# A Fourier layer with routed experts on one core: selection per batch, loads ahead of their use, folds two steps ahead, paired tiles

## The chip, the cores and the metric

The kernel runs on one core of a Trainium2 chip. The metric is the device time of one execution in microseconds (us); lower is better. Five engines work side by side, each in its own program order: TensorE (PE, with its weight loads shown as PEld), VectorE (DVE), ScalarE (ACT), GpSimd (POOL) and SyncE (SP), which here issues nearly all DMAs.

## The reference

There are 8 batches of 3136 rows of 256 numbers. Per batch:

```python
X = np.fft.rfft(x, axis=1)                 # along the 3136 rows
Yr = Xr @ w_r - Xi @ w_i + b_r
Yi = Xr @ w_i + Xi @ w_r + b_i
Y  = sign(Y) * max(abs(Y) - 0.01, 0)       # on Yr and Yi
y  = np.fft.irfft(Yr + 1j * Yi, n=3136, axis=1)
scores = y @ w_gate                        # one score a row
top = the 128 rows of the batch with the highest scores
y[top] += sigmoid(scores[top]) * (relu(y[top] @ w1) @ w2)   # w1 256x1024, w2 1024x256
```

## The kernel before

The transform of 3136 = 98 x 32 rows is done as two stages of matmuls with a pass through scratch memory between them, and so is the inverse. The units of work are these:

- `ld_x`, `fold`, `s1`: a batch comes in 8 groups. `ld_x` loads a group into one of four fixed tiles `xt` (batch 0 also uses the tiles `cv`), `fold` adds and subtracts its two halves into `sd` (POOL; every other group of batch 0 on DVE), `s1` runs the 98-point matmuls into the PSUM tile `s`, ACT copies that to `at`, and three DMAs store it to the scratch `As`.
- `ld_a`, `s2`: a batch has 13 frequency groups. `s2` runs the 32-point matmuls into `px`; ACT rounds the result to `Xh` (line 425) and DVE makes the rest `Xl` (line 426).
- `spectral`: the product of X and the weights in three real products of six matmuls each. The first, called k1, goes to one half of the PSUM tile `pc`; ACT copies it to `ks` (line 441), POOL adds the bias to give `kb` (line 443), and DVE adds `kb` to the other two products in `py` (line 446).
- `shrink` makes `Y` from `py` (ACT line 451, DVE line 453).
- `s2i`: the inverse 32-point matmuls, also into `pc` (line 470). ACT copies the result to `ct` (line 474), and two DVE operations reduce it against the gate (`junk`, line 477), which gives the part `Csc` of the scores. The result is stored to the scratch `Cs`.
- `ld_c`, `s1i`: 8 groups a batch, loaded from `Cs` into four tiles `cv`, matmuls into `s`, a copy to `ot` on ACT and three DMAs to the output.
- Routing: `score` makes a batch's scores, `select` finds the 128th highest by a search over the bits of the numbers, and `place` turns the threshold into 128 row numbers `idx`. One turn of the search compares all scores with several candidates (`c`, line 232), counts (`n`, line 237), sums over partitions by a matmul into the upper half of `pc` (`tot`, line 240), and updates the threshold by four small DVE operations (`ok`, `d`, `w`, `f`).
- Experts: `gather` fetches the 128 rows by an indirect DMA on POOL, `prepare`, `hidden` and `combine` run the two expert matmuls, and a second indirect DMA on POOL writes the rows back. This is called FFN below.

Every engine's order is written by hand. One loop runs over t, one spectral group a step; t = 0 to 103 are the 104 groups of the 8 batches. In step t the program emits, in this order: stores left from the step before; the loads; `s2` of group t+1; the first of the step's `s1`/`s1i` pairs (`s1` is 17 groups ahead, `LEAD`, and `s1i` 17 behind, `LAG`); one tick of the routing threads; `spectral` of t; the folds for the next step's `s1`; one tick of the FFN; `s2i` of t-1; `shrink` of t; a second pair if there is one; and a second tick of the routing threads. A tick runs each thread (a generator) to its next `yield`. After the last step the threads are ticked until they end.

Routing has four threads: batches 0 to 3 are selected together, then 4 and 5, then 6, then 7. A thread of several batches begins its search when the last of them has its scores. The search takes two bits a turn for several batches, with two ticks a turn, and three bits with one tick for a single one. The expert weights w2 come in 8 parts, one every second step from t = 22: a part is loaded and, in the same step, rounded by ACT (`w2h`, line 199) and split by POOL. Ahead of the loop stands a prelude: the loads of batch 0 and of the spectral weights, the splitting of those weights on DVE (`consts_a`), the 8 folds and `s1` of batch 0, and 50 matmuls that only keep TensorE busy (`warm`).

Of the kernel before, what the change touches and what calls it, by code (L numbers as in the profile page):

```python
# [23 lines left out]
NF = 64  # L24
# [76 lines left out]
def fourier_moe(ctx: ExitStack, tc: tile.TileContext, x, w_r, w_i, b_r, b_i, wg, w1, w2,  # L101
# [20 lines left out]
    xts, cvs = [[c_tile([128, 4, D], F32, n + str(k)) for k in range(4)] for n in ("xt", "cv")]  # L122
    for t in xts + cvs:
        nc.gpsimd.memset(t[32:64], 0.0)
    nc.scalar.dma_start(out=w, in_=t_w)
    g_sb = c_tile([128, NJ - 1, 3 * N2], F32, "g_sb")
    gt_sb = c_tile([NF, 3, NF], F32, "gt_sb")
    wts = [[c_tile([128, 2, D], F32R, n + c) for c in "hl"] for n in ("ws", "wd", "wn")]
    xth, xtl = [c_tile([128, 2, 3, 128], F32R, n) for n in ("xth", "xtl")]
# [15 lines left out]
    digits = c_tile([N1, 256], U32, "digits")  # L145
# [4 lines left out]
    route_ps = pc[:, 1, D:]  # L150

    def consts_a():
# [3 lines left out]
        ld(wi, w_i.rearrange("(h p) e -> p h e", p=128))  # L156

# [31 lines left out]
    def consts_b():  # L189
        ld(wq, t_wq)  # L190
        make_identity(nc, ident)

    def consts_moe(k):
        if k == 0:
            ld(w1s, w1.rearrange("(h p) f -> p h f", p=128))
        elif k <= FF // 128:
            t = pool.tile([128, D], F32, name="xe", bufs=3)
            ld(t, w2[128 * k - 128:128 * k])
            nc.scalar.copy(out=w2h[:, k - 1, :], in_=t)
            nc.gpsimd.tensor_tensor(out=w2l[:, k - 1, :], in0=t, in1=w2h[:, k - 1, :].bitcast(F32), op=ALU.subtract)  # L200
        else:
            ld(digits, t_dig)
            nc.gpsimd.dma_start(out=tm, in_=t_m)
            nc.gpsimd.iota(iota, [[1, 128 * NCHK]], base=0, channel_multiplier=0, allow_small_or_imprecise_dtypes=True)
            nc.gpsimd.iota(nrow, [[1, 1]], base=0, channel_multiplier=N2, allow_small_or_imprecise_dtypes=True)
            nc.gpsimd.iota(tcol, [[128, NCHK]], base=0, channel_multiplier=1, allow_small_or_imprecise_dtypes=True)
# [6 lines left out]
    def select(bs, bits, thrs):  # L213
        nb = bs.stop - bs.start
        tag = f"_{bs.start}"
        sv = scores[:, bs, :].rearrange("p b (o c) -> p b o c", o=1)
# [4 lines left out]
        for hi, i in zip([32] + cuts, cuts):  # L221
            m = 2 ** (hi - i) - 1
            f = pool.tile([N1, nb, m], U32, name="f" + tag, bufs=1)
            if w is None:
                nc.vector.memset(f, 0)
            else:
                nc.vector.tensor_tensor(out=f, in0=digits[:, 8 * i:8 * i + m].rearrange("p (o m) -> p o m", o=1).broadcast_to([N1, nb, m]),
                                        in1=w.broadcast_to([N1, nb, m]), op=ALU.bitwise_xor)
            if nb > 1:
                yield  # L230
            c = pool.tile([N1, nb, m, N2], BF16, name="c" + tag, bufs=1)
            nc.vector.tensor_tensor(out=c, in0=sv.broadcast_to([N1, nb, m, N2]),  # L232
                                    in1=f.bitcast(F32).rearrange("p b (m o) -> p b m o", o=1).broadcast_to([N1, nb, m, N2]),
                                    op=ALU.is_ge)
            n = pool.tile([N1, nb, m], BF16, name="n" + tag, bufs=1)
            with nc.allow_low_precision(reason="counts up to 28 are exact"):
# [4 lines left out]
            w2 = pool.tile([N1, nb, 1], U32, name="w" + tag)  # L241
            if w is None:
                nc.vector.tensor_scalar(out=w2.bitcast(I32), in0=tot, scalar1=cap - 0.5, scalar2=1.0, op0=ALU.is_ge, op1=ALU.subtract)
            else:
                d = pool.tile([N1, nb, 1], U32, name="d" + tag, bufs=1)
                if m == 1:
                    nc.vector.tensor_scalar(out=d, in0=tot, scalar1=cap - 0.5, scalar2=None, op0=ALU.is_ge)
                else:
                    ok = pool.tile([N1, nb, m], F32, name="ok" + tag, bufs=1)
# [5 lines left out]
        for b in range(bs.start, bs.stop):  # L255
            thrs[b] = w.bitcast(F32)[:, b - bs.start, :]

    def place(b, thr, slots):
# [4 lines left out]
        yield  # L263
        pt = route_ps[:2 * N2, :N1]
        nc.tensor.matmul(pt, mf, eye, start=True, stop=True)
        mt = pool.tile([2 * N2, N1], BF16, name="mt")
        nc.vector.tensor_copy(mt, pt)
        yield
# [6 lines left out]
        for a in range(2):  # L275
            nc.vector.tensor_copy(row[:, a, N2 + 1:], nrow)
        yield
# [6 lines left out]
        for k in range(NCHK):  # L284
# [7 lines left out]
            yield  # L292
# [11 lines left out]
            slots[b, k] = idx  # L304

# [54 lines left out]
    def ld_x(b, i):  # L360
        t = xt[b, i] = (cvs if b == 0 and i > 3 else xts)[i % 4].rearrange("p (h c) d -> p h c d", h=2)
        for r in range(2):
            ld(t[64 * r:64 * r + 48], xv[b, :48, :, 4 * i + 2 * r:4 * i + 2 * r + 2, :])
        ld(t[48:113:64], xv[b, 48, :, 4 * i:4 * i + 4, :].rearrange("h (r c) d -> r h c d", r=2))

    def fold(b, i):
        t = xt.pop((b, i)).rearrange("p h c d -> p h (c d)")
        f = sd[b, i] = pool.tile([128, 2, 2 * D], F32, name="sd", bufs=2)
        for k, op in enumerate((ALU.add, ALU.subtract)):
            (nc.vector if b == 0 and i % 2 else nc.gpsimd).tensor_tensor(out=f[:113, k], in0=t[:113, 0], in1=t[:113, 1], op=op)  # L370

    def s1(b, i):
        if i == 0:
            As[b] = dram.tile([2, NH, N2, D], F32, name="As")
        f = sd.pop((b, i))
        p = ps.tile([128, 2, 2 * D], F32, name="s", bufs=1)
        for r in range(2):
            for c in range(2):
                nc.tensor.matmul(p[64 * c:64 * c + 64, r, :], w[64 * r:64 * r + NH, c, :], f[64 * r:64 * r + NH, c, :], start=True, stop=True)  # L379
        t = pool.tile([128, 4, D], F32, name="at", bufs=3)  # L380
        nc.scalar.copy(out=t.rearrange("p (r c) d -> p r (c d)", r=2), in_=p)  # L381

        def store():
            for q in range(2):
                nc.sync.dma_start(out=As[b][q, :48, 4 * i:4 * i + 4, :], in_=t[64 * q:64 * q + 48])
            nc.sync.dma_start(out=As[b][:, 48, 4 * i:4 * i + 4, :], in_=t[48:113:64])
        stores.append(store)

    def ld_a(b, g):
        if g == G - 1:  # L390
            av[b, g] = pool.tile([64, 1, D], F32, name="av", bufs=3)
# [295 lines left out]
```

## Time and profile before

| | us |
|---|---|
| median of 3 runs | 1042.05 (1038.84 to 1045.21) |
| the profiled execution's own time | 1035.69 |
| its span | 1033.9 |

| engine | busy share of the span | instructions |
|---|---|---|
| PE | 76% | 7540 |
| PEld | 54% | 7540 |
| DVE | 43% | 1275 |
| ACT | 36% | 579 |
| POOL | 30% | 268 |

The busy shares are means over stretches with different limits, so they do not say what a change to one stretch is worth. The granted clock of TensorE over the execution was 0.892 of 2.4 GHz; at each moment it is either 1.2 or 2.4 GHz. `kb` (line 443) runs once in each of the 104 steps, so counting it counts steps.

### The profile page before, as it was taken

What the parts mean: (1) busy time and instruction counts of PE and PEld (TensorE: products, weight loads), DVE (VectorE), ACT (ScalarE), POOL (GpSimd) and SP (SyncE); (2) the same over time, 40 slices, a digit from 0 to 9 for tenths busy, and PEclk for the clock granted to TensorE, in tenths of its full rate; (3) what the DMA queues carried; (4) which work ended last, traced back from release to release, by engine and by line L of the source; (5) the groups of instructions that cost most, each with busy time, mean ns of one, the idle gap of its engine ahead of it and who ended that gap; (6) DMA issues with size and microseconds to landing.
All of it is one profiled execution on the core that took longest, in us unless ns stands there. A gap on an engine that the chain in (4) does not pass through costs nothing. (4 is left out here: it accounts for less than half of the span.)

```text
span 1033.9 us, 19572 instructions
## 1 busy us (share of the span) xinstructions
PE 782.4 (76%) x7540; PEld 557.1 (54%) x7540; DVE 447.1 (43%) x1275; ACT 369.7 (36%) x579; POOL 312.6 (30%) x268
## 2 busy tenths in 40 slices
PE   1589998965865789988777878678878766677675
PEld 0066666643643466666555655466556655564364
DVE  1214454522322344543555454544554466544521
ACT  0214453523433345553443343433443222223211
POOL 5125644423322353433333233331411110111011
PEclk9999999987888799998899798997998877888799
DMA  8378967875675687997685576864553334315520
GB/s 182 93 184 206 242 175 172 262 196 139 154 180 140 160 216 203 251 246 179 162 212 160 130 191 171 215 162 110 154 154 95 98 99 114 88 52 142 165 60 21
DMA packets 104762, 163.69 MB, mean 158 GB/s; under 512 B 12161, under 2 KB 65502, under 8 KB 104670
## 3 DMA queue, kind: packets, MB, share of 16 engines
q1 hardware_dynamic: 103630, 160.18, 59.7%
q0 software_dynamic: 896, 2.17, 0.7%
q8 instruction: 60, 0.98, 0.4%
q14 instruction: 32, 0.26, 0.1%
q10 hardware_dynamic: 144, 0.10, 0.0%
HBM read 84.35 MB, written 78.12 MB: 157 GB/s over the span
## 5 line engine op out<-in xcount | busy, mean ns | idle before, releaser
L443 POOL TENSOR_TENSOR kb<-ks,bias 128x512 f32<-128x512 f32 (+1 forms) x104 | 132.8, 1277 | 513.2 <-ACT ks L441 497.9
L446 DVE TENSOR_TENSOR py<-py,kb 128x512 f32<-128x512 f32 (+1 forms) x104 | 72.7, 699 | 256.9 <-POOL kb L443 176.4
L370 POOL TENSOR_TENSOR sd<-xt 113x512 f32<-113x512 f32 x116 | 145.1, 1272 | 21.0 <-DMA xt<-in_x 18.7
L470 PE MATMUL pc<-Y,gi_sb 64*128 64x256 f32 x768 | 119.2, 432 | 39.5 <-ACT ks L441 39.5
L474 ACT COPY ct<-pc 128x512 f32<-128x512 f32 (+1 forms) x104 | 59.0, 568 | 244.1 <-PE pc L470 221.2
L379 PE MATMUL s<-sd,w 49*64 49x512 f32 x512 | 112.3, 721 | 42.5 <-POOL sd L370 15.4
L426 DVE TENSOR_TENSOR Xl<-px,Xh 128x768 fp32r<-128x768 f32 x96 | 91.5, 953 | 111.0 <-ACT Xh L425 110.8
L477 DVE CUSTOM_DVE_ANT_0 junk<-pc,wgb 128x256 f32<-128x256 f32 (+1 forms) x200 | 84.8, 424 | 89.6 <-ACT ct L474 86.2
L470 PEld LDWEIGHTS pc<-Y,gi_sb 64*128 64x128 f32 x768 | 72.6, 205 | 59.8 <-ACT ks L441 40.7
L209 PE MATMUL pc<-wsh,Xh 128*128 128x256 f32 x192 | 68.3, 355 | 41.1 <-DVE ok L250 17.7
L418 PEld LDWEIGHTS px<-g_sb,av 64*64 64x64 f32 x3072 | 79.3, 144 | 36.7 <-issue 29.6
L425 ACT CAST Xh<-px 128x768 fp32r<-128x768 f32 x96 | 76.9, 801 | 59.4 <-PE px L418 59.2
L418 PE MATMUL px<-g_sb,av 64*64 64x96 f32 x3072 | 95.1, 264 | 2.0 <-DVE Xl L426 1.9
L381 ACT COPY at<-s 128x1024 f32<-128x1024 f32 x64 | 65.0, 1015 | 77.7 <-PE s L379 76.5
L209 PEld LDWEIGHTS pc<-wsh,Xh 128*128 128x128 f32 x192 | 39.2, 204 | 93.2 <-issue 33.5
L441 ACT COPY ks<-pc 128x256 f32<-128x256 f32 (+1 forms) x104 | 38.8, 373 | 111.0 <-PE pc L211 109.6
L507 PE MATMUL s<-cv,w 49*64 49x512 f32 x480 | 74.2, 669 | 2.7 <-ACT ot L509 2.5
L509 ACT COPY ot<-s 128x1024 f32<-128x1024 f32 x64 | 64.8, 1012 | 31.7 <-PE s L507 26.7
L451 ACT ACTIVATE r<-py,m2l 128x512 f32<-128x512 f32 (+1 forms) x104 | 71.8, 690 | 2.5 <-DVE py L446 2.5
L453 DVE SCALAR_TENSOR_TENSOR Y<-py,r 128x512 f32<-128x512 f32 (+1 forms) x104 | 71.3, 686 | 1.9 <-ACT r L451 1.9
L379 PEld LDWEIGHTS s<-sd,w 49*64 49x64 f32 x512 | 22.9, 152 | 80.2 <-POOL sd L370 44.8
L209 PE MATMUL py<-wdh,Xh 128*128 128x256 f32 x192 | 60.5, 315 | 0.0
(139 smaller groups left out, 1365.7 us busy)
## 6 DMA issues: line engine op xcount, KB each, us to landing
As<-at SPq DMA_DIRECT2D x128, 192.0 KB
av<-As SPq DMA_DIRECT2D x96, 256.0 KB
Cs<-ct SPq DMA_DIRECT2D x48, 512.0 KB
out<-ot SPq DMA_DIRECT2D x128, 192.0 KB
xt<-in_x SPq DMA_DIRECT2D x120, 192.0 KB
cv<-Cs SPq DMA_DIRECT2D x120, 192.0 KB
cv<-in_x SPq DMA_DIRECT2D x8, 192.0 KB
gi_sb<-t_gi SPq DMA_DIRECT2D x6, 256.0 KB
```

Source lines behind the costliest of these rows:

```text
L209: nc.tensor.matmul(out, wh, mh, start=start, stop=False)
L370: (nc.vector if b == 0 and i % 2 else nc.gpsimd).tensor_tensor(out=f[:113, k], in0=t[:113, 0], in1=t[:113, 1], op=op)
L379: nc.tensor.matmul(p[64 * c:64 * c + 64, r, :], w[64 * r:64 * r + NH, c, :], f[64 * r:64 * r + NH, c, :], start=True, stop=True)
L418: nc.tensor.matmul(o[:, :, N2 * j:N2 * j + N2], a[64 * p:64 * p + 64, 2 * (g % 2) + j, 128 * h + 64 * q:128 * h + 64 * q + 64], g_sb[64 * ...
L425: nc.scalar.copy(out=vh, in_=v)
L426: nc.vector.tensor_tensor(out=vl, in0=v, in1=vh.bitcast(F32), op=ALU.subtract)
L443: nc.gpsimd.tensor_tensor(out=kb[:r], in0=ks[:r].broadcast_to([r, 2, D]), in1=bias[:r], op=ALU.add)
L446: nc.vector.tensor_tensor(out=py[:r], in0=py[:r], in1=kb[:r], op=ALU.add)
L451: nc.scalar.activation(out=r1[:r], in_=py[:r], func=AF.Relu, bias=m2l[:r], scale=1.0)
L470: nc.tensor.matmul(p[:, q, :], gi_sb[64 * q:64 * q + 64, g, c, :], y[64 * q:64 * q + 64, c, :], start=(c == 0), stop=(c == 1))
L477: nc.vector.tensor_tensor_reduce(out=junk[:r], in0=p[:r, k, :], in1=wgb[:r], scale=1.0, scalar=0.0, op0=ALU.mult, op1=ALU.add, accum_out=C ...
L507: nc.tensor.matmul(p[64 * c:64 * c + 64, r, :], w[64 * r:64 * r + NH, 2, :], f[64 * r:64 * r + NH, 2 * c:2 * c + 2, :], start=True, stop=True)
```

## The change

- Routing has one thread a batch. The search takes four bits a turn (15 candidates) with one turn a step: in a step's first tick the matmul `tot` and the small operations, in its second the compare and the count. `place` and `score` also move one stage a step, always in the first tick. The second tick moves from the end of the step into `spectral`, between k1 and the other two products.
- In `pc`, k1 and the routing change places, and the selection has columns of its own beside those of the rest of the routing.
- The parts of w2 are loaded from t = 14 on, and rounded and split four steps after their load.
- Folds stand two steps ahead of their `s1`, not one.
- `ld_x`, `ld_c` and the stores of `s1` and `s1i` handle two groups at once: tiles are twice as large and half as many, each DMA moves twice as much, and there are half as many DMAs. The `av` tiles go from three to two.
- In batch 0, `s1` alternates between the PSUM tiles `s` and `px`, `at` tiles are joined by `ot` tiles, and DVE does the folds of all groups but the third and the sixth. The weights are split after the folds. `warm` has 30 matmuls.
- `s2i` is cut into matmuls of 64 x 64 weights (twice as many). `LAG` is 18.

The core of the diff (the parts of `s1i` and `ld_c` are like those of `s1` and `ld_x`, and `place` gains a second `yield` at each of its own):

```diff
-    def select(bs, bits, thrs):
+    def select(b, bits, thrs):
...
-            if nb > 1:
-                yield
+            yield
...
+            c = pool.tile([N1, m, N2], BF16, name=f"c{m}")
+            nc.vector.tensor_tensor(out=c, in0=sv.broadcast_to([N1, m, N2]),
+                                    in1=f.bitcast(F32).rearrange("p (m o) -> p m o", o=1).broadcast_to([N1, m, N2]), op=ALU.is_ge)
...
             yield
-            tot = route_ps[:N1, :nb * m].rearrange("p (b m) -> p b m", b=nb)
+            tot = sel_ps[:N1, :m]
             nc.tensor.matmul(tot, ones, n, start=True, stop=True)
...
-    route_ps = pc[:, 1, D:]
+    sel_ps, route_ps = pc[:, 0, D:D + 64], pc[:, 0, D + 64:]
...
-        k1 = pc[:, 0, D:]
+        k1 = pc[:, 1, D:]
...
+        between()
         product(py[:, 0, :], 1, wts[2])
         product(py[:, 1, :], 0, wts[1])
...
-    def route(bs, bits):
-        for b in range(bs.start, bs.stop):
-            while done["s2i"] < b:
-                yield
+    def route(b):
+        while done["s2i"] < b:
             yield
-            yield from score(b)
             yield
-        yield from select(bs, bits, thrs)
-        for b in range(bs.start, bs.stop):
-            yield from place(b, thrs[b], slots)
-            yield
+        yield
+        yield
+        yield from score(b)
+        yield from select(b, 4, thrs)
+        yield from place(b, thrs[b], slots)
...
-    threads = [route(slice(0, 4), 2), route(slice(4, 6), 2), route(slice(6, 7), 3), route(slice(7, 8), 3)]
+    threads = [route(b) for b in range(B)]
...
+        if 0 <= k < FF // 128:
+            w2t[k] = pool.tile([128, D], F32, name="xe", bufs=3)
+            ld(w2t[k], w2[128 * k:128 * k + 128])
+
+    def split_moe(k):
+        if 0 <= k < FF // 128:
+            t = w2t.pop(k)
+            nc.scalar.copy(out=w2h[:, k, :], in_=t)
+            nc.gpsimd.tensor_tensor(out=w2l[:, k, :], in0=t, in1=w2h[:, k, :].bitcast(F32), op=ALU.subtract)
...
     def ld_x(b, i):
-        t = xt[b, i] = (cvs if b == 0 and i > 3 else xts)[i % 4].rearrange("p (h c) d -> p h c d", h=2)
+        if i % 2:
+            return
+        k = i // 2
+        t = xt[b, k] = (cvs if b == 0 and k > 1 else xts)[k % 2].rearrange("p (h c) d -> p h c d", h=2)
...
-        p = ps.tile([128, 2, 2 * D], F32, name="s", bufs=1)
+        p = ps.tile([128, 2, 2 * D], F32, name="px" if b == 0 and i % 2 else "s", bufs=1)
...
+        nc.scalar.copy(out=t[:, :, i % 2, :], in_=p)
+        if i % 2 == 0:
+            return
...
-            av[b, g] = av[b, g + 1] = pool.tile([128, 4, D], F32, name="av", bufs=3)
+            av[b, g] = av[b, g + 1] = pool.tile([128, 4, D], F32, name="av", bufs=2)
...
+        if w == 2:
+            for c in range(2):
+                for q in range(2):
+                    for a in range(2):
+                        nc.tensor.matmul(p[64 * a:64 * a + 64, q, :], gi_sb[64 * q:64 * q + 64, g, c, 64 * a:64 * a + 64], y[64 * q:64 * q + 64, c, :],
+                                         start=(c == 0), stop=(c == 1))
...
-        for i in range(50):
+        for i in range(30):
...
-    LEAD, LAG = 17, 17
+    LEAD, LAG = 17, 18
...
     for i in range(U):
-        fold(0, i)
+        fold(0, i, nc.gpsimd if i % 3 == 2 else nc.vector)
         s1(0, i)
         flush()
+    weights()
     warm()
...
-        for b, i in steady(t + LEAD + 3):
+        for b, i in steady(t + LEAD + 4):
             ld_x(b, i)
...
-        if t in range(20, 20 + 2 * (FF // 128 + 2), 2):
-            consts_moe((t - 20) // 2)
+        if t % 2 == 0:
+            consts_moe((t - 14) // 2)
+            split_moe((t - 18) // 2)
...
         if 0 <= t < B * G:
-            py, r = spectral(*divmod(t, G))
-        for b, i in steady(t + LEAD + 1):
-            fold(b, i)
+            py, r = spectral(*divmod(t, G), lambda: tick(threads))
+        else:
+            tick(threads)
+        for b, i in steady(t + LEAD + 2):
+            fold(b, i, nc.gpsimd)
...
         pair()
-        tick(threads)
```

## Rows read from the trace of the kernel before

**Rows 1.** Windows, `kb` alone: stretch, length, busy (steps), granted clock, DMA share, GB/s.

```profile
0.00:71.70 71.70, 0.00 (x0) 1.00 0.67 151
71.70:166.60 94.90, 19.19 (x15) 0.98 0.79 199
166.60:202.90 36.30, 7.67 (x6) 1.00 0.83 225
202.90:376.00 173.10, 22.88 (x18) 0.82 0.66 170
376.00:466.90 90.90, 17.92 (x14) 0.98 0.86 229
466.90:577.40 110.50, 16.62 (x13) 0.89 0.69 178
577.40:942.00 364.60, 48.54 (x38) 0.86 0.49 129
942.00:1034.00 92.00, 0.00 (x0) 0.85 0.33 94
```

**Rows 2.** Timeline of the prelude: start, length, engine, line, tiles; idle before, its releaser.

```profile
22.64 0.43 DVE L159 CAST wsh<-r 128x512 fp32r<-128x512 f32 x1 [22.64 <-DMA r<-in_w_r]
...
35.27 1.98 PE L379 MATMUL s<-sd,w 49*64 49x512 f32 x8 [1.12 <-ACT at L381]
...
51.76 13.97 PE L524 MATMUL px<-Xh 128*128 128x512 f32 x50 [1.69 <-ACT Xh L521]
```

**Rows 3.** Timeline of POOL over two early steps.

```profile
84.38 1.27 POOL L443 TENSOR_TENSOR kb<-ks,bias 128x512 f32<-128x512 f32 x1 [2.58 <-ACT ks L441]
85.61 2.50 POOL L370 TENSOR_TENSOR sd<-xt 113x512 f32<-113x512 f32 x2
90.69 1.27 POOL L443 TENSOR_TENSOR kb<-ks,bias 128x512 f32<-128x512 f32 x1 [2.57 <-ACT ks L441]
95.84 1.28 POOL L443 TENSOR_TENSOR kb<-ks,bias 128x512 f32<-128x512 f32 x1 [3.89 <-ACT ks L441]
```

**Rows 4.** Waits: who waited for whom, us in total, times, longest.

```profile
ACT w2h L199 <- DMA xe<-in_moe_w: 58.1, 8, 10.3
```

**Rows 5.** Timeline of one step with a turn of the search in it.

```profile
521.08 1.14 PE L470 MATMUL pc<-Y,gi_sb 64*128 64x256 f32 x8
521.59 0.70 DVE L446 TENSOR_TENSOR py<-py,kb 128x512 f32<-128x512 f32 x1 [2.27 <-POOL kb L443]
...
523.05 0.84 PE L418 MATMUL px<-g_sb,av 64*64 64x96 f32 x32
...
523.70 0.69 DVE L453 SCALAR_TENSOR_TENSOR Y<-py,r 128x512 f32<-128x512 f32 x1
...
524.30 0.55 DVE L232 TENSOR_TENSOR c<-scores,f 98x384 bf16<-98x384 f32 x1
...
525.35 0.95 DVE L426 TENSOR_TENSOR Xl<-px,Xh 128x768 fp32r<-128x768 f32 x1
...
526.21 0.16 DVE L250 TENSOR_SCALAR ok<-pc 98x12 f32<-98x12 f32 x1
...
526.43 0.39 PE L209 MATMUL pc<-wsh,Xh 128*128 128x256 f32 x1 [0.78 <-DVE ok L250]
...
528.74 1.13 PE L470 MATMUL pc<-Y,gi_sb 64*128 64x256 f32 x8
```

**Rows 6.** Lines by form: the compare of the search on fewer numbers.

```profile
L232 DVE TENSOR_TENSOR c<-scores,f 98x224 bf16<-98x224 f32 x20 | 7.8, 392 | 0.7
```

**Rows 7.** Timeline of the last FFN.

```profile
1018.23 1.00 POOL L353 DMA_INDIRECT out<-ye,idx  x1 [9.45 <-DVE ye L352]
...
1018.97 2.05 PE L334 MATMUL m<-xT,w1s 128*128 128x128 f32 x16 [0.52 <-DVE xT L319]
...
1029.19 0.48 DVE L352 SCALAR_TENSOR_TENSOR ye<-m,ga,xe 128x256 f32<-128x256 f32 x1 [3.23 <-PE m L211]
...
1029.95 0.98 POOL L353 DMA_INDIRECT out<-ye,idx  x1 [10.72 <-DVE ye L352]
```

More of the change, by code (lines that the diff above doesn't have):

```diff
@@ L156, in consts_a, with weights @@
         ld(wi, w_i.rearrange("(h p) e -> p h e", p=128))
+        for c, src in enumerate((b_r, b_i)):
+            ld(bias[:, c, :], src.rearrange("(o e) -> o e", o=1).broadcast_to([128, D]))
+        w3[:] = wr, wi, wt
+    def weights():
+        wr, wi, wt = w3
         def parts(t, pair):
@@ L211, in mm3 @@
         return nc.tensor.matmul(out, wh, ml, start=False, stop=stop).ins
[L213 to L216 removed]
+    def select(b, bits, thrs):
+        sv = scores[:, b:b + 1, :]
         cuts = [31]
@@ L254, in select @@
             w = w2
-        for b in range(bs.start, bs.stop):
-            thrs[b] = w.bitcast(F32)[:, b - bs.start, :]
+        thr = pool.tile([N1, 1], F32, name=f"thr{b}", bufs=1)
+        nc.vector.tensor_copy(thr, w.bitcast(F32))
+        thrs[b] = thr
+        yield
+        yield
     def place(b, thr, slots):
@@ L402, in s2 @@
         px = ps.tile([128, 2, 512], F32, name="px", bufs=1)
+        xh, xl = [pool.tile([128, 2, 3, 128], F32R, name=n, bufs=XB) for n in ("Xh", "Xl")]
+        X[b, g] = xh, xl
         if w == 1:
+            for t in (xh, xl):
+                nc.gpsimd.memset(t[:, :, :, NF:].bitcast(F32), 0.0)
             for h in range(2):
@@ L421, in s2 @@
                                          start=True, stop=True)
-        xh, xl = [pool.tile([128, 2, 3, 128], F32R, name=n, bufs=XB) for n in ("Xh", "Xl")]
         v = px[:, :, :384].rearrange("p a (k j s) -> p a k j s", k=6, j=2)
@@ L426, in s2, with spectral @@
         nc.vector.tensor_tensor(out=vl, in0=v, in1=vh.bitcast(F32), op=ALU.subtract)
-        X[b, g] = xh, xl
-    def spectral(b, g):
+    def spectral(b, g, between):
         r = 128 if width(g) == 2 else NF
@@ L466, in s2i @@
         p = pc[:, :, :D]
-        for c in range(2):
-            for q in range(w):
-                if w == 2:
-                    nc.tensor.matmul(p[:, q, :], gi_sb[64 * q:64 * q + 64, g, c, :], y[64 * q:64 * q + 64, c, :], start=(c == 0), stop=(c == 1))
-                else:
-                    nc.tensor.matmul(p[:64, 0, :], gti_sb[:, c, :], y[:64, c, :], start=(c == 0), stop=(c == 1))
+        if w == 2:
[5 more added lines that the diff above has]
+        else:
+            for c in range(2):
+                nc.tensor.matmul(p[:64, 0, :], gti_sb[:, c, :], y[:64, c, :], start=(c == 0), stop=(c == 1))
         o = 2 * (g % 2)
@@ L490, in score @@
         yield
+        yield
         p = route_ps[:N1, :N2]
@@ L602, in fourier_moe @@
     ld_x(1, 0)
-    ld_x(1, 1)
-    fold(1, 0)
+    ld_x(1, 2)
+    fold(1, 0, nc.gpsimd)
+    fold(1, 1, nc.gpsimd)
     for t in range(-1, B * G + LAG + 1):
         flush()
-        for b, i in steady(t + LEAD + 3):
+        for b, i in steady(t + LEAD + 4):
             ld_x(b, i)
-        if t + 2 in first and first[t + 2] > 1:
+        if t + 2 in first and first[t + 2] > 2:
             ld_x(1, first[t + 2])
@@ L641, in fourier_moe @@
         if 0 <= t < B * G:
-            py, r = spectral(*divmod(t, G))
-        for b, i in steady(t + LEAD + 1):
-            fold(b, i)
-        if t + 1 in first and t >= 0:
-            fold(1, first[t + 1])
+            py, r = spectral(*divmod(t, G), lambda: tick(threads))
+        else:
+            tick(threads)
+        for b, i in steady(t + LEAD + 2):
+            fold(b, i, nc.gpsimd)
+        if t + 2 in first and t >= 0:
+            fold(1, first[t + 2], nc.gpsimd)
         tick(ffns)
```

129 lines of the change are left out of this document (68 added, 61 removed).

## The prediction

> **What bounds the kernel now.** First I cut the span into stretches and count steps in each by the 104 runs of `kb` [rows 1]. The reader should see that the pace differs: a step takes 94.9/15 = 6.3 us at the start, 6.05 in the next six, 173.1/18 = 9.6 in the stretch to 376, 90.9/14 = 6.5 up to 467, 110.5/13 = 8.5 in the next and 364.6/38 = 9.6 in the long one after it. Ahead of the steps stand 71.7 us, behind them 92. The granted clock is near 1.00 where steps are short and 0.82 to 0.89 where they are long. So no single engine sets the time; each stretch has its own chain, and I looked for it in the timeline of each.
>
> The prelude: DVE's first act waits 22.64 us for a spectral weight, and DVE's share of the folds stands behind the splitting. From then on a group costs 1.98 us of matmuls and about 1.1 of waiting until ACT has emptied the one PSUM tile `s`; then `warm` takes 13.97 [rows 2]. Early steps: `kb` to `kb` is 6.31 us with a fold between and 5.15 without [rows 3]; the fold sits between this step's `kb` and the `s1` that the next step's k1 must follow, so POOL is in the chain. In the stretch to 376, ACT waits eight times, 58.1 us in all, for a part of w2 [rows 4], and everything behind it on ACT waits too. From 467 on, a step with a turn of the search has this chain [rows 5]: `s2i`, then ACT's copy and DVE's two reductions, `Y` at 2.62 us after the start of `s2i`, `c` and `n`, `Xl` (0.95), `ok`, and only then k1, since k1 waits for the last DVE reader of `pc` and DVE works in order. From k1 it is 2.31 us to the next `s2i`: 7.66 us in all.
>
> **The change part by part.** t is the step, as in the code; the sum is made against the span of 1033.9.
>
> Prelude. DVE's folds no longer stand behind the weights, and two PSUM tiles take away the wait for ACT; a fold on DVE comes from the loads instead. x arrives in 12 larger DMAs rather than 24. At 151 to 199 GB/s [rows 1] its 3.2 MB take 16 to 21 us, so I let the eight `s1` end at about 25. The splitting on DVE, now behind the folds, ends near 30, `warm` is 30/50 of 13.97 = 8.4, and the first `kb` followed `warm` by 6.0 us (51.76 + 13.97 to 71.7 [rows 1, 2]): 30 + 1 + 8.4 + 6 = about 46; I take 47, with 42 (clock high early, loads at the upper rate) and 55 (loads at the lower rate, the stores to `As` late).
>
> Steps 0 to 14. With the fold a step earlier the 6.31 steps become like the 5.15 ones. The traffic of the stretch, 199 GB/s x 94.9 us = 18.9 MB, at 5.4 us a step would run at 233 GB/s, which 376 to 466.9 already reached (229). 15 x 5.4 = 81 us, from 77 (5.15) to 86.
>
> The weights of w2. Loaded four steps, some 25 us, ahead, they land before they are rounded: the longest wait is 10.3 us [rows 4]. ACT's copy and POOL's split stay, under a microsecond each, off the chain. The cost at nothing rests on the SP queue; were it late by as much as now, 58 us would stay.
>
> The search. Four bits make 15 candidates, 480 numbers a partition. `c` is 0.39 us at 224 and 0.55 at 384 [rows 5, 6], so 0.65 at 480; `n` the same. They now run behind `ok` and ahead of `py`, where DVE waits 2.27 us for POOL [rows 5]; the three small operations behind `ok` at some 0.2 each and `c` and `n` at 1.35 take about 2.0 there. So DVE does more work in all, and 1.05 us leaves the chain: 7.66 - 1.05 = 6.6. If POOL's cover were gone, the 1.3 would come back. What is late next is `ok` behind `Xl`, as now. In 3 of 13 steps both an `s1` and an `s1i` are due (7 of 13 with `LAG` 17); the second one pushes `Xl` by about 0.8, so 0.2 on average. The route of a batch takes about 18 steps of the 13 between batches, so in 5 steps of 13 two threads tick together and put 0.3 to 0.9 us of `place` and `score` before k1: 0.2 on average. 7.0 us a step at full clock, from t = 15 on. No matmul of the routing stands at the step's end ahead of the next `s2` any more.
>
> FFN. An FFN is 2 x 2.05 us of `hidden`, about 2.9 of `combine` (DVE's wait for it is 3.23) and 0.4 of transposes [rows 7]: some 7.4 us of PE between the products and `s2i`, spread over 7 of 13 steps, 0.6 a step. It is in the chain. Batch b has its rows at t = 13b + 32, so FFNs run from t = 35 on and seven of the eight are done before the loop ends, where now four end behind it. 7.6 a step from t = 35.
>
> The clock. At 0.89 the search steps of 467 to 577 average 8.5 against 7.66 at full clock: 11% for 0.11. In the step of rows 5 k1 waits 0.78 and `tot` before it waits for `n` as well. In a new step 3.2 us lie between the end of `s2i` and k1, and PE has an `s2` (0.84) and mostly one `s1` (1.0, at full clock half of rows 2) to fill them; a wait of about 1.1 is left, less than now. So I take 0.93 and add 7%: 7.5 for the 20 steps to t = 34, 8.1 for the 69 from 35 to 103. 150 + 559 us. Bounds: full clock (7.0, 7.6) and 0.82, the lowest stretch of rows 1 (8.3, 9.0). The Trainium skill, page "TensorE: Matmul & The Clock Gate", Part 1, says that the throttled clock is the default and activity releases it; rows 1 agree (1.00 and 0.98 where steps are shortest). By that rule it speaks against this change, which puts a short wait of PE into every step from 15 on instead of half of them; with 0.82 throughout the sum would be 78 us higher.
>
> Fewer and larger DMAs, two `av` tiles, the quadrant form of `s2i`: nothing, since loads stand two steps ahead of their use, the pair's stores still land two steps before `As` is read, and an `s2i` of the same columns on four quadrants instead of two halves has the same work. Bounds: a saving of 0.1 us a step, or a load late by 2 us for each of the 32 pairs, 64 us.
>
> The end. The last four FFNs, at 11.7 us each [rows 7], make about 47 of the 92 us behind the steps. After: the route of batch 7 is 3 steps of scores, 9 turns and 6 stages of `place`. A turn is `tot`, four small operations, `c` and `n`: 2.4 us alone, 3 (my estimate) with the `s1i` and FFN matmuls between: 27 for the turns, and at 1.8 a stage some 16 for the scores and `place`: 43. Then one FFN (11.7), and a gather and a scatter at 3 and 4 us (the last scatter is issued at 1029.95, 4 us before the end; the gather is taken a little below it): 62 from the last scores, which come some 2 us before the stretch begins. So it falls from 92 to about 60 (52 to 75).
>
> Sum: 47 + 81 + 150 + 559 + 60 = 897 of span, 1.8 outside it (1035.69 - 1033.9): 899. The median of the runs stands 0.6% above the profiled execution: 905 us.
>
> **The rivals.**
> - The pace stays. The chain through DVE is not shortened, because `c` and `n` push `py`, or the clock stays at 0.82 to 0.86. At 8.3 to 8.5 for 20 steps and 9.0 to 9.3 for 69: 47 + 81 + 168 + 631 + 62 = 989, or 997 as a median. For it: DVE's busy time rises by about 50 us. Against it: DVE is idle 2.27 us just where the work goes.
> - The end is not shortened, because one turn a step makes batch 7's route 18 steps long: 92 us stay, 937. For it: its selection still starts after the last scores. Against it: its chain is shorter than the three FFNs that go away.
> - The w2 wait moves and does not vanish: 58 us more, 963.
> - Slower: with a routing tick ahead of k1 in every step, PE falls to half clock and stays there. Then k1 to `s2i` (2.31) and `s2i` (1.1) double, 10.4 us a step and 12 with FFN: 47 + 81 + 208 + 828 + 75 = 1239. It decides from a mean of (1034 - 47 - 81 - 62)/89 = 9.5 us a step, which needs a clock below about 0.7; no stretch of rows 1 is below 0.82.
>
> **How the numbers follow.** Forecast 0.64 (its own range 855 to 950), pace 0.18, end 0.10, w2 0.04, slower 0.04. The range that leaves out no more than 2 in 10 goes from 860, with nearly full clock and the lower bounds of prelude and end, to 985, which takes in the end, w2 and half of the pace rival. A measurement of this kernel tells about 0.5% from no change. Faster by over that 0.95, within it 0.01, slower 0.04.
>
> **What would show it.** Right: first `kb` at 42 to 55 us; `kb` to `kb` about 5.2 in the first 15 steps; no ACT wait for w2; in search steps `c` and `n` between `ok` and `py`, and 6.6 to 7.7 us a step; a granted clock over 0.9; one gather behind the last output store. Wrong: DVE's `py` waiting for `n` and not POOL; k1 waiting over 1.5 us a step for `ok`; SP waiting for a fold, `s2` or `s1i` before a load, or folds waiting for x, which would show pairs to be too coarse.

## The result, and the profile after

The changed kernel takes 905.87 us (median of 4 runs, 904.73 to 909.62) against 1040.44 for the kernel before in the same runs (4 runs, 1037.69 to 1045.21): a ratio of 0.871, 95% interval 0.867 to 0.875. The forecast was 905. The profiled execution took 905.22 us with a span of 903.4.

The windows of the changed kernel, cut at the forecast's terms (the columns of [rows 1]; `kb` is now line 467):

```profile
0.00:54.30 54.30, 0.00 (x0) 0.88 0.91 196
54.30:144.60 90.30, 19.17 (x15) 0.92 0.90 212
144.60:289.30 144.70, 25.59 (x20) 0.94 0.90 218
289.30:827.00 537.70, 88.32 (x69) 0.95 0.74 174
827.00:903.40 76.40, 0.00 (x0) 0.67 0.50 115
```

| stretch | forecast | bounds | measured | difference |
|---|---|---|---|---|
| prelude, to the first `kb` | 47 | 42 to 55 | 54.3 | +7 |
| steps 0 to 14 | 81 | 77 to 86 | 90.3 | +9 |
| steps 15 to 34 | 150 | 140 to 166 | 144.7 | -5 |
| steps 35 to 103 | 559 | 524 to 621 | 537.7 | -21 |
| end | 60 | 52 to 75 | 76.4 | +16 |
| span | 897 | | 903.4 | +6 |

So the total is right to 0.1%, but by luck: three terms are 7 to 16 us too small (32 together) and two are 26 us too large, and two of the five (90.3 against 86, 76.4 against 75) lie outside their bounds. The misses cancel but for 6 us, and the 0.6% that the forecast put on top for the median covers nearly all of those; here the median stands only 0.07% above the profiled execution.

A step with a turn of the search, in the timeline of the changed kernel (answers to [rows 5]):

```profile
383.35 0.16 DVE L254 TENSOR_SCALAR ok<-pc 98x15 f32<-98x15 f32 x1
...
383.57 0.39 PE L218 MATMUL pc<-wsh,Xh 128*128 128x256 f32 x1 [1.33 <-DVE ok L254]
...
384.15 0.66 DVE L237 TENSOR_TENSOR c<-scores,f 98x480 bf16<-98x480 f32 x1
...
384.85 0.66 DVE L241 TENSOR_REDUCE n<-c 98x15 bf16<-98x480 bf16 x1
...
385.87 1.09 PE L496 MATMUL pc<-Y,gi_sb 64*64 64x256 f32 x16
...
386.38 0.70 DVE L471 TENSOR_TENSOR py<-py,kb 128x512 f32<-128x512 f32 x1 [0.88 <-POOL kb L467]
...
386.79 0.84 PE L444 MATMUL px<-g_sb,av 64*64 64x96 f32 x32
...
388.47 0.69 DVE L478 SCALAR_TENSOR_TENSOR Y<-py,r 128x512 f32<-128x512 f32 x1
...
389.07 0.95 DVE L451 TENSOR_TENSOR Xl<-px,Xh 128x768 fp32r<-128x768 f32 x1
389.94 0.16 DVE L254 TENSOR_SCALAR ok<-pc 98x15 f32<-98x15 f32 x1
...
390.15 0.38 PE L218 MATMUL pc<-wsh,Xh 128*128 128x256 f32 x1 [1.34 <-DVE ok L254]
```

From `ok` to `ok` it is 6.59 us, where 6.6 were forecast. This is the plain step: of 49 such distances in the loop, 20 are at most 6.84, and the rest, where other work is added, go up to 9.12 (median 7.1). `c` and `n` (0.66 each, forecast 0.65) run between `ok` and `py`, and `py` still waits 0.88 for POOL's `kb`: the cover for them exists. The k1 product waits 1.33 us for `ok`, and `ok` stands right behind `Xl`.

The waits of the changed kernel hold no wait of ACT for w2 ([rows 4]: 58.1 us before):

```profile
PE pc L218 <- DVE ok L254: 59.2, 55, 1.5
POOL sd L387 <- DMA xt<-in_x: 48.7, 4, 23.9
```

Before, the second one was a single wait:

```profile
POOL sd L370 <- DMA xt<-in_x: 18.7, 1, 18.7
```

Three of the four are now batch 1's (the fourth, 10.4 us, is the first of batch 0). POOL's timeline, three rows out of the prelude and the early steps (answers to [rows 3]), shows where it falls:

```profile
47.81 4.92 POOL L387 TENSOR_TENSOR sd<-xt 113x512 f32<-113x512 f32 x4 [23.90 <-DMA xt<-in_x]
...
75.60 2.48 POOL L387 TENSOR_TENSOR sd<-xt 113x512 f32<-113x512 f32 x2 [5.18 <-DMA xt<-in_x]
...
93.47 2.48 POOL L387 TENSOR_TENSOR sd<-xt 113x512 f32<-113x512 f32 x2 [9.23 <-DMA xt<-in_x]
```

Folds of batch 1 wait for x: the first ones until 47.81, and two more in steps 3 and 5, which take 8.9 and 13.0 us from `kb` to `kb`. The other 13 early steps take 68.4 us, 5.3 each (forecast 5.4).

PE's timeline of the prelude (answers to [rows 2]), its last `s1` of batch 0, `warm` and the first `s1` of batch 1:

```profile
27.07 1.44 PE L398 MATMUL px<-sd,w 49*64 49x512 f32 x8
...
33.59 9.00 PE L564 MATMUL px<-Xh 128*128 128x512 f32 x30 [5.09 <-ACT Xh L561]
...
49.13 3.20 PE L398 MATMUL s<-sd,w 49*64 49x512 f32 x8 [2.78 <-POOL sd L387]
```

The `s1` end at 28.5 (forecast 25), `warm` takes 9.0 (8.4), and the first k1 has to follow an `s1` that waits for a fold that waits for x.

The end, in the timeline of the changed kernel (answers to [rows 7]):

```profile
828.35 0.07 DVE L505 DVE_READ_ACCUMULATOR2_ANT Csc<- 64x1 f32 x1
...
836.09 0.06 DVE L232 MEMSET f<- 98x1 uint32 x1
...
839.94 0.16 DVE L247 TENSOR_SCALAR w<-pc 98x1 int32<-98x1 f32 x1 [2.76 <-PE pc L244]
...
867.53 0.15 DVE L260 COPY thr<-w 98x1 f32<-98x1 f32 x1
...
878.86 0.15 DVE L314 TENSOR_TENSOR idx<-col,pc 128x1 uint32<-128x1 f32 x1
...
882.77 0.96 POOL L322 DMA_INDIRECT xe<-out,idx  x1 [6.88 <-DMA out<-ot]
...
886.79 3.79 PE L347 MATMUL m<-xT,w1s 128*128 128x128 f32 x16 [0.52 <-DVE xT L332]
...
899.48 1.00 POOL L366 DMA_INDIRECT out<-ye,idx  x1 [15.74 <-DVE ye L365]
```

The last scores `Csc` come at 828.4, batch 7's rows `idx` at 879.0, so its route takes 50.6 us (forecast 43): 31.6 for the nine turns (836.1 to 867.7, forecast 27) and 19.0 for the scores and `place` (forecast 16). The gather then waits 3.8 more for the last output stores, which the forecast had not put in. From gather to scatter it is 16.7 (forecast 14.7): the first half of `hidden` runs at half clock (0.50 granted), 3.79 instead of 2.05.

### The profile page after: what moved, and what is told of

Same layout as the page of the kernel before. It is cut to its first block, busy times and chain, and to the rows that moved or that the text cites. A ratio compares the mean times of both kernels' runs of the same rounds, so it can differ in the third digit from the quotient of the medians.

```text
span 903.4 us, 20480 instructions
## 1 busy us (share of the span) xinstructions
PE 700.4 (78%) x8302; PEld 516.7 (57%) x8302; DVE 501.2 (55%) x1369; ACT 365.2 (40%) x579; POOL 309.3 (34%) x272
## 4 chain that ended last, share of the span: by engine, by line
PE 43%; DVE 19%; ACT 9%; DMA 5%; issue 5%; POOL 1%; SPq 1%; POOLq 0%; ACTq 0%
PE pc L496 8%; DVE Xl L451 6%; DVE junk L505 6%; PE pc L218 5%; PE py L218 5%; PE py L219 5%; PE py L220 5%; ACT ct L502 4%; DVE Y L478 4%; PE m L347 3%; PE s L544 3%; PE pc L220 2%; PE pc L219 2%; ACT ot L546 2%; DMA cv<-Cs 2%
## 5 line engine op out<-in xcount | busy, mean ns | idle before, releaser
L218 PE MATMUL pc<-wsh,Xh 128*128 128x256 f32 x208 | 74.1, 356 | 90.2 <-DVE ok L254 59.2
L218 PEld LDWEIGHTS pc<-wsh,Xh 128*128 128x128 f32 x208 | 42.9, 206 | 124.4 <-DVE ok L254 61.7
L496 PE MATMUL pc<-Y,gi_sb 64*64 64x256 f32 x1536 | 106.1, 392 | 0.0
L444 PEld LDWEIGHTS px<-g_sb,av 64*64 64x64 f32 x3072 | 78.9, 134 | 29.9 <-issue 13.5
L444 PE MATMUL px<-g_sb,av 64*64 64x96 f32 x3072 | 85.4, 245 | 9.8 <-DMA av<-As 7.2
L398 PE MATMUL s<-sd,w 49*64 49x512 f32 x480 | 74.6, 647 | 20.7 <-DVE sd L387 10.4
L544 PE MATMUL s<-cv,w 49*64 49x512 f32 x480 | 71.5, 631 | 10.7 <-ACT ot L546 8.2
L400 ACT COPY at<-s 128x1024 f32<-128x1024 f32 x58 | 59.7, 1030 | 22.9 <-PE s L398 22.9
L496 PEld LDWEIGHTS pc<-Y,gi_sb 64*64 64x64 f32 x1536 | 49.9, 134 | 25.6 <-issue 2.4
L218 PE MATMUL py<-wnh,Xh 128*128 128x256 f32 x208 | 63.9, 307 | 0.0
L220 PE MATMUL py<-wnl,Xh 128*128 128x256 f32 x208 | 63.9, 307 | 0.0
```

Of the source, the lines that this page charges most:

```text
L218: nc.tensor.matmul(out, wh, mh, start=start, stop=False)
L220: return nc.tensor.matmul(out, wh, ml, start=False, stop=stop).ins
L444: nc.tensor.matmul(o[:, :, N2 * j:N2 * j + N2], a[64 * p:64 * p + 64, 2 * (g % 2) + j, 128 * h + 64 * q:128 * h + 64 * q + 64], g_sb[64 * ...
L496: nc.tensor.matmul(p[64 * a:64 * a + 64, q, :], gi_sb[64 * q:64 * q + 64, g, c, 64 * a:64 * a + 64], y[64 * q:64 * q + 64, c, :], start=(c ...
```

## Experiments

All medians are over 4 to 6 runs. Kernels are compared by their ratio to the kernel before, measured beside each of them; the changed kernel stands at 0.871 (0.867 to 0.875).

**e1: x earlier.**

```diff
-        if t + 2 in first and first[t + 2] > 2:
-            ld_x(1, first[t + 2])
+        if t + 4 in first and first[t + 4] > 2:
+            ld_x(1, first[t + 4])
```

> The changed kernel, but the third and fourth pair of x of batch 1 are loaded two steps earlier (steps 1 and 3, not 3 and 5). Theory: in the changed kernel these loads stand in the step of their own fold, POOL waits 5.2 and 9.2 us for them, kb queues behind, and steps 3 and 5 take 8.9 and 13.0 us; both waits go, steps 3 and 5 take 5 to 6, and the time falls by 10 to 12 us to about 895. Rival: the DMA engines are full there (0.90 busy), so the wait only moves to another load: within 3 us of 906.

Measured: 901.33 us, ratio 0.867 (0.860 to 0.874). The windows:

```profile
0.00:56.50 56.50, 0.00 (x0) 0.86 0.88 193
56.50:138.30 81.80, 19.20 (x15) 0.97 0.96 230
```

The 15 steps fall from 90.3 to 81.8 us, the forecast's 81: the two waits are the whole miss of that term. The first `kb` comes 2.2 us later in this execution, at 56.5; without this edit it lies between 53.0 and 55.9 (e6, e7), and in e9, which has the same edit, at 54.4, so this is not put down to it. In the total the intervals overlap; a gain is not shown.

**e2: w2 late.** Each part of w2 is loaded in the step in which it is rounded, as before; w1, which is loaded with the first part, comes four steps later too.

```diff
-            consts_moe((t - 14) // 2)
+            consts_moe((t - 18) // 2)
```

> The changed kernel, but each part of w2 is loaded in the step that rounds it, as before the change. Theory: ACT waits again for each of the 8 parts, 6 to 7 us a time, with everything behind it: 945 to 965 us. Rival: the steps are longer now and the load would be hidden anyway: under 920.

Measured: 988.13 us, ratio 0.951 (0.946 to 0.958), 82 us slower than the changed kernel; more than expected. The window of steps 15 to 34:

```profile
144.80:368.20 223.40, 25.63 (x20) 0.78 0.61 141
```

The waits of this kernel, two lines:

```profile
POOL w2l L215 <- ACT w2h L214: 76.1, 8, 16.6
ACT w2h L214 <- DMA xe<-in_moe_w: 64.7, 8, 14.2
```

Nearly all of the loss is in steps 15 to 34: 223.4 against 144.7. ACT's eight waits give 64.7 of it. POOL waits behind ACT with `kb` and folds queued behind it, and the clock of the stretch falls from 0.94 to 0.78.

**e3: the second tick at the end of the step.**

```diff
-            py, r = spectral(*divmod(t, G), lambda: tick(threads))
-        else:
-            tick(threads)
+            py, r = spectral(*divmod(t, G), lambda: None)
...
         pair()
+        tick(threads)
```

> The changed kernel, but the second routing tick stands at the end of the step again; the compare and the count then lie between Y and Xl on DVE. Theory: their 1.32 us come back into the chain of the 63 to 72 steps that have a turn: 65 to 90 us more, 970 to 995, less in steps with two pairs, where Xl waits for ACT anyway. Rival: PE or POOL sets the step and DVE's order does not matter: under 925.

Measured: 1028.19 us, ratio 0.990 (0.983 to 0.997). Nearly the whole gain is gone. The windows:

```profile
145.40:314.20 168.80, 25.64 (x20) 0.88 0.80 188
314.20:949.00 634.80, 88.36 (x69) 0.87 0.63 148
```

8.44 us a step, then 9.20, against 7.23 and 7.79. These are the paces of the prediction's first rival (8.3 to 8.5 and 9.0 to 9.3): `c` and `n` go back into the chain, and the clock falls to 0.87. In its waits `tot` now waits for `n`:

```profile
PE pc L244 <- DVE n L241: 106.0, 56, 3.5
```

**e4: Xl behind the first routing tick.** In step t, `Xl` is made for group t+1, so the products that read it come a step later; DVE's `Xl` is now emitted after that tick.

```diff
-        nc.vector.tensor_tensor(out=vl, in0=v, in1=vh.bitcast(F32), op=ALU.subtract)
+        late.append(lambda: nc.vector.tensor_tensor(out=vl, in0=v, in1=vh.bitcast(F32), op=ALU.subtract))
...
         pair()
         tick(threads)
+        while late:
+            late.pop(0)()
```

> The changed kernel, but the DVE operation that makes Xl is emitted after the first routing tick, not ahead of it. Theory: k1 waits for ok, and ok only for Xl (0.95 us) in DVE's order; Xl is not needed before the next step, so k1 starts up to 0.95 us earlier in some 85 steps: 840 to 860 us, k1's wait for ok under 0.5 us a step. Rival: TensorE's own work (with FFN and throttled clock) is the next bound right behind: 885 to 906.

Measured: 839.91 us, ratio 0.808 (0.803 to 0.813), faster than both kernels. The timeline of a search step:

```profile
363.44 0.16 DVE L254 TENSOR_SCALAR ok<-pc 98x15 f32<-98x15 f32 x1
...
363.66 0.39 PE L218 MATMUL pc<-wsh,Xh 128*128 128x256 f32 x1 [0.47 <-DVE ok L254]
...
364.13 0.95 DVE L451 TENSOR_TENSOR Xl<-px,Xh 128x768 fp32r<-128x768 f32 x1
...
369.41 0.39 PE L218 MATMUL pc<-wsh,Xh 128*128 128x256 f32 x1 [0.47 <-DVE ok L254]
```

A step is 5.75 us instead of 6.59. The wait of k1 falls from 1.33 to 0.47: `ok` no longer stands behind an operation that nobody needs before the next step.

**e5: the kernel before, with only its w2 parts loaded ahead.** The rounding and the split of each part come four steps behind its load (`split_moe`, as in the change).

> The kernel before, with one part of the change alone: each part of w2 is loaded in the same steps as before, but ACT rounds it and POOL splits it four steps later. Theory: ACT's eight waits, 58.1 us in all, lie in the chain of every second step and go away, so 50 to 65 us less than before, about 980. Leaving this part out of the changed kernel cost 82 us, more than the sum of its waits, so up to 80 us less is possible. Rival: the other waits of those steps (the loads of group pairs, the two-batch search turns) take the place of half of it: 25 to 35 us less, about 1008.

Measured: 981.07 us, ratio 0.941 (0.936 to 0.946): 61 us less than 1042.21 for the kernel before. The theory holds.

**e6: folds one step ahead.**

```diff
-        for b, i in steady(t + LEAD + 2):
+        for b, i in steady(t + LEAD + 1):
...
-        if t + 2 in first and t >= 0:
-            fold(1, first[t + 2], nc.gpsimd)
+        if t + 1 in first and t >= 0 and first[t + 1] > 1:
+            fold(1, first[t + 1], nc.gpsimd)
```

In this kernel one fold of the 64, group 5 of batch 1, reads the pair that is loaded over its own, and has to wait for that load.

> The changed kernel with folds one step ahead of their s1, as before. Theory: in the early steps that have a fold the next k1 follows an s1 that waits for the fold, 1.16 us each as between 6.31 and 5.15 us before, 7 of the first 15 steps: 8 us more. In search steps k1 is held by ok some 3 us behind s2i, longer than the fold takes, so nothing more there: 912 to 916. Rival: in the search steps too the s1 waits for the fold, in 8 of 13 steps by about 1 us: 50 us more, about 955. Second rival: the x loads of the early steps are the limit whichever step the fold stands in: within 4 us of 906.

Measured: 912.73 us, ratio 0.879 (0.873 to 0.885): 7 us more. In its trace the early steps with a fold take 6.3 us, as in [rows 3], and the 15 take 95.9 us (53.00 to 148.91) instead of 90.3. Plain search steps stay at 6.6 to 6.8. The theory's steps of 6.3 us are there, but the sum mixes two effects: nine such steps cost more, and of the changed kernel's two waits of early folds for x (5.18 and 9.23) neither is left, only one of 4.37 us for the load over group 5's pair, in a step of 12.6 us. So the price of the fold alone is not shown, and the interval overlaps that of the changed kernel.

**e7: s2i in 64 x 128 weights.**

```diff
-                    for a in range(2):
-                        nc.tensor.matmul(p[64 * a:64 * a + 64, q, :], gi_sb[64 * q:64 * q + 64, g, c, 64 * a:64 * a + 64], y[64 * q:64 * q + 64, c, :],
-                                         start=(c == 0), stop=(c == 1))
+                    nc.tensor.matmul(p[:, q, :], gi_sb[64 * q:64 * q + 64, g, c, :], y[64 * q:64 * q + 64, c, :], start=(c == 0), stop=(c == 1))
```

> The changed kernel with s2i in 8 matmuls of 64x128 weights as before. Theory (the prediction took nothing): the same columns at the same rate, 1.14 against 1.09 us, and 0.05 us a step is 5 us at most: 903 to 911. Rival: between s2i and the s2 behind it PE stands idle when the weights change shape (before, s2 started 0.83 us behind the end of s2i; now it starts as s2i ends), and as s2 is no longer ahead of k1's wait for ok by much, a part of this shows: 0.1 to 0.3 us a step, 915 to 935.

Measured: 915.28 us, ratio 0.879 (0.875 to 0.883): 9 us more, between the two. The timeline of this kernel, `s2i` and the `s2` behind it:

```profile
387.54 1.13 PE L495 MATMUL pc<-Y,gi_sb 64*128 64x256 f32 x8
...
388.61 0.89 PE L444 MATMUL px<-g_sb,av 64*64 64x96 f32 x32
```

`s2` starts 1.07 us behind the start of `s2i`, in the changed kernel 0.92. In the plain search steps only 0.04 us a step of it shows (6.63 us from `ok` to `ok`); over steps 35 to 86 it is 0.06 a step (7.94 against 7.88), 3 us. Steps 87 to 103 take 7.92 us each instead of 7.53, but in e1, where `s2i` is as in the changed kernel, they take 7.91 too. So where the rest of the 9 us lies is not settled, and the intervals of the two kernels meet at 0.875.

**e8: LAG 17.** One constant.

> The changed kernel with LAG at 17. Theory: 7 instead of 3 of 13 steps hold two of s1 and s1i, the second stands behind shrink and its ACT copy is ahead of the next Xh; Xl, ok and k1 come some 0.8 us later in four more of 13 steps, 89 x 4/13 x 0.8 = 22 us more, and the end is one step (7 us) shorter: 915 to 925. Rival: those steps hold the wait anyway and other steps get shorter in return, so that only the end counts: 897 to 902.

Measured: 923.31 us, ratio 0.886 (0.881 to 0.891): 17 us more. The theory holds: the end is 79.6 us from the last `kb` (851.03 to 930.6), against 84.1, but the steps from 35 to 86 take 8.25 us each instead of 7.88. Counted by the place of a step in its 13, the five that gain a second pair are 0.6 to 2.3 us longer there, and the one that loses it is 0.8 shorter. The profiled execution, at 932.42, is the slowest of the six.

**e9: e1 and e4 together.**

> The changed kernel with both e1's and e4's edits: batch 1's last x pairs two steps earlier, Xl behind the first routing tick. Theory: the two act in different stretches (early steps; steps from 15 on) and add up: 839.9 - 4.5 = 835, 832 to 839. Rival: the earlier loads only move the wait to the next x pair or the prelude, and nothing of the 4.5 is left: 838 to 843.

Measured: 832.11 us, ratio 0.797 (0.793 to 0.802), the fastest. Steps 0 to 14 take 82.7 us and the steps from 15 on keep e4's pace, so the two add up.

**e10: without the FFN of batch 6.**

> The changed kernel without the gather, the expert matmuls and the scatter of batch 6, so that batch 6's best rows keep their values without the experts' part. Theory: the end is 16 us longer than forecast because batch 6 too has its rows only behind the loop (13 x 6 + 32 = 110, past 103), so that its FFN stands on PE between batch 7's inverse matmuls and search turns, most of it at half clock: 10 to 15 us less, 891 to 896, all of it behind the last kb. Rival: batch 7's route and output stores set the end, and this FFN fills waits: within 3 us of 906.

Measured: 902.91 us, ratio 0.868 (0.863 to 0.872). The theory falls: the FFN in the end is worth about 3 us, within what can be told from nothing. From its last `kb` (822.52) this kernel's end takes 78.3 us, against 84.1 in the changed kernel and 81.7 in e1, whose end is the same. The timeline of its end shows why so little comes of it:

```profile
829.99 0.07 DVE L505 DVE_READ_ACCUMULATOR2_ANT Csc<- 64x1 f32 x1
...
873.77 0.15 DVE L314 TENSOR_TENSOR idx<-col,pc 128x1 uint32<-128x1 f32 x1
...
879.03 0.98 POOL L322 DMA_INDIRECT xe<-out,idx  x1 [43.33 <-DMA out<-ot]
```

Without this FFN batch 7's route takes 43.9 us, near the forecast's 43, and not 50.6 (47.1 to 50.7 in the other kernels here). But the gather then waits 5.1 us for the last output stores, and from gather to scatter (896.99) it is 18.0 us and not 16.7. The rival is right that batch 7's route and the output stores set the end; that the FFN only fills waits is not so, since the route is longer with it.

**e11: extra matmuls in the end.**

```diff
         pair()
+        if t >= B * G:
...
+            for i in range(2):
+                nc.tensor.matmul(pad[:, i, :], wts[0][0][:, 0, :128], wts[0][0].rearrange("p h d -> p (h d)"), start=True, stop=True)
```

> The changed kernel with two matmuls of 128x512 that nobody reads, ahead of the first routing tick in each step from 104 on (19 steps). Theory: the end's granted clock of 0.67 makes each s1i last 1.97 instead of 1.04 us and each quarter of hidden 2.05 instead of 1.03; the extra 38 matmuls, 0.25 us each, close PE's waits, the clock rises over 0.85 and 8 s1i and 6 quarters get 1 us shorter each, against up to 9 us of added matmuls: 896 to 905. Rival: the clock stays near 0.67 and the matmuls cost 10 to 15 us: 916 to 921.

Measured: 904.69 us, ratio 0.869 (0.866 to 0.872), no difference. Two windows of this kernel's end (busy us of PE, PEld, DVE, ACT and POOL, granted clock, DMA share, GB/s), from 20.6 us behind its last `kb` on:

```profile
844.02:874.02 30.00, 25.95 (x122) 14.81 (x118) 17.32 (x58) 7.48 (x9) 0.97 (x1) 0.65 0.66 148
874.02:905.30 31.28, 15.44 (x94) 11.99 (x92) 5.94 (x22) 2.41 (x4) 2.97 (x3) 0.84 0.17 45
```

The same windows of the changed kernel, then of e7, which adds no matmuls there:

```profile
840.00:870.00 30.00, 21.78 (x94) 11.09 (x94) 18.04 (x59) 7.30 (x9) 0.97 (x1) 0.50 0.67 142
870.00:903.40 33.40, 16.16 (x102) 12.97 (x98) 6.42 (x25) 3.42 (x5) 2.96 (x3) 0.76 0.20 53
...
850.73:880.73 30.00, 21.83 (x115) 11.27 (x108) 17.51 (x59) 7.47 (x9) 0.97 (x1) 0.64 0.66 147
880.73:912.40 31.67, 14.13 (x80) 11.80 (x78) 5.69 (x21) 2.41 (x4) 2.96 (x3) 0.69 0.16 42
```

The granted clock of the first window, 0.65, is above the changed kernel's 0.50, but e7 has 0.64 there without the added matmuls, so no rise is shown in it. In the second it is 0.84 against 0.76 and 0.69. The time does not change. What the clock alone costs here stays open.

**e12: e9, with the first x loads of batch 1 ahead of the load of `As`.**

```diff
         flush()
+    ld_x(1, 0)
+    ld_x(1, 2)
     weights()
     warm()
...
-    ld_x(1, 0)
-    ld_x(1, 2)
```

> The kernel of e9 with the loads of batch 1's first two x pairs moved ahead of the load of As in SP's order. Theory: the prelude is over its forecast because SP waits for the stores to As before it issues these loads (39.5 us), so the folds of batch 1 wait for x until 47.8 and the first k1 behind its s1; with the loads at 34.6 the first kb comes 3 to 5 us earlier, at 49 to 51, and the time is 827 to 830. Rival: the loads take the SP queue and the bandwidth of the first av, s2 comes 3 us later in return, and the first kb stays at 53 to 57: 831 to 835.

Measured: 837.22 us, ratio 0.805 (0.802 to 0.809), a little slower than e9. The timeline of its prelude:

```profile
42.42 4.92 POOL L387 TENSOR_TENSOR sd<-xt 113x512 f32<-113x512 f32 x4 [18.87 <-DMA xt<-in_x]
...
48.29 0.58 PE L444 MATMUL px<-g_sb,av 64*64 64x96 f32 x4 [5.85 <-DMA av<-As]
...
58.49 1.28 POOL L467 TENSOR_TENSOR kb<-ks,bias 128x512 f32<-128x512 f32 x1 [11.15 <-ACT ks L465]
```

x comes 5.4 us earlier than in e9 (47.78 there), and in return `s2` starts at 48.29 instead of 42.32 and the first `kb` at 58.49 instead of 54.35. The rival's mechanism holds, at a higher price. The loads of `av` are issued 3.1 us later than in e9 (39.28 against 36.15), and `s2` starts 6.0 later, so the order on SP is a part of it and not the whole. Of these two orders, whichever load is put first, the other one holds k1. The Trainium skill, page "Trainium Kernel Development and Optimization", section "Key Constraints", says that DMAs issued from the SP, ACT and POOL queues all run on the same 16 DMA engines and interleave. Here SP issues both loads, so no run tests this for several queues; the DMA share of this prelude is 0.95 (0.91 in e9).

## Why the prediction was right, point by point

**The search step: right.** 6.59 us against 6.6. e3 shows the reason: with the second tick back at the end the pace is the rival's, 8.44 and 9.20. The place of `c` and `n` is worth 122 us here, more than 1.32 us times the 63 turns of the first seven batches (83 us). The granted clock falls with it, from 0.95 to 0.87; how much of the other 39 us that makes was not separated.

**The wait of k1: right in place.** Forecast about 1.1 us behind `ok`, which stands behind `Xl`; measured 1.33. e4 moves `Xl` alone and takes 0.84 us from the step and 66 us from the kernel.

**w2: right.** No wait of ACT for it is left. Both directions were run: 61 us gained on the kernel before (e5), 82 lost when taken back in the changed one (e2). e2 and e3 give back 204 us together, more than the 135 gained; so the two prices overlap or the rest of the change costs time without them. Which of these it is was not run.

**The paces: right, sized a little too high.** 7.23 and 7.79 us against 7.5 and 8.1. The clock was 0.94 to 0.95, not 0.93; at the prediction's own rate of 1% for 0.01 that is some 7.6 x 1.05 = 8.0, so it explains about a third of the 21 us; the rest is not attributed. The clock rule weighed against the change (a short wait of PE in every step) did not come to pass: k1 waits for `ok` in 55 steps, 59.2 us in all, and the granted clock is above the 0.82 to 0.89 of before.

**Steps 0 to 14: mis-sized by 9 us.** The step that failed is that larger and fewer DMAs cost nothing because loads stand two steps ahead of their use. For two pairs of batch 1 they do not: the change moved the folds one step up but not these loads, so each stands in the step of its own fold. They were late by 5.18 and 9.23 us. With the folds back a step (e6) neither of these waits is there; with the loads two steps earlier (e1) the term falls to 81.8. So the lead was missing, and that the size of the DMAs costs time is not shown.

**The prelude: mis-sized by 7.** `s1` and `warm` ended 3 to 4 us late, and from the end of `warm` (42.6) to the first `kb` it took 11.8 us instead of the 6.0 carried over from before. The 5.8 are batch 1's first folds, which wait for x until 47.81. e12 shows that the other order of these loads gains nothing: what x wins, `av` loses.

**The end: mis-sized by 16.** "Seven of the eight FFNs are done before the loop ends" is false by the prediction's own formula: rows of batch b come at t = 13b + 32, so batch 6 has them at 110 and batch 5's scatter comes at 833.04, behind the last `kb`. By e10 this error costs about 3 us in all, though 3 to 7 in the route (47.1 to 50.7 against 43.9): without batch 6's FFN the last output stores, which the sum left out, hold the gather. The 16 are the sum of four terms in the timeline: the last scores come 1.4 us into the stretch and not 2 ahead of it (3.4), the route takes 50.6 and not 43 (7.6, nearly all of it gone in e10), the gather waits for the last stores (3.8), and the last FFN runs partly at half clock (2.0). That the others would go away by themselves was not shown; e11's attempt on the clock gave nothing. The 1.8 us a stage of scores and `place` in the sum were read from no row; the nine stages took 2.1 each.

**The small edits.** The quadrant form of `s2i` was costed at nothing; without it the median is 9 us higher (e7), of which the trace shows 3 in the steps it bears on. `LAG` 18 is worth 17 (e8), near the 0.8 us a second pair that the prediction used. Without the earlier folds it is 7 us more (e6), but mixed with other waits for x. Larger DMAs, two `av` tiles and the alternation of `s` and `px` in batch 0 were not taken back by themselves.

**What stays open.** k1 writes the half of `pc` that `tot` and `ok` do not use, and yet it waits for `ok`. The Trainium skill, page "PSUM — Partial Sum Buffer", section "PSUM bank collisions raise a hardware error", asks for a guard by bank and quadrant; its section "Specifications (TRN2)" gives 2 KiB a bank, 512 float32, which is a half of `pc`. By that rule k1 would need only the reads of its own half, by `junk` and by ACT's copies. The trace shows the wider wait (1.33 us, 0.47 in e4); two tiles of one bank each in place of `pc` were not tried.

## What to carry to other kernels

Find in the timeline which instruction of an in-order engine stands just ahead of the one that releases the bottleneck, and ask whether it has to be there: moving `c` and `n` was worth 122 us here, moving `Xl` another 66. A load that arrives too late on an engine that others queue behind cost at least its waits here (64.7 us of waits and 78.7 of time in e2, 58.1 and 61 in the kernel before), so put loads of constants several steps ahead. A sum that comes out right in total is not a sum whose terms are right: cut the profile at the terms before you believe it.

## What the runs showed of the hardware

- The granted clock was 0.94 to 0.95 over 89 steps, in 55 of which k1 waits for `ok` (59.2 us in all, 1.5 at most). In 30 us of the end, in which PE alternates `s1i` and FFN matmuls with waits for DVE's turns, it was 0.50, and 0.64 in e7 with the same work there. With 38 added matmuls (e11) it was 0.65, and the time did not change.
- A `s2i` on 64 x 128 weights delayed the 64 x 64 matmuls behind it by 0.15 us against the same columns on 64 x 64 weights, in the steps shown (1.07 against 0.92). In e7 weight loads of `s2` wait for their own issue 36.7 us over 100 times, 13.5 over 31 in the changed kernel.
- The two ways to order half a batch of x (1.6 MB) and the first `av` (e9, e12) move the first `kb` by 4 us (54.35 and 58.49), with a DMA share of 0.91 and 0.95 in the prelude.
